# Reciprocals of three chunks spread by way of DRAM, and one tile transposed by DMA, in a fused attention and GEGLU kernel

## The chip, the cores and the metric

The kernel runs on one core of a Trainium2 chip. The metric is the device time of one execution in microseconds, as the median of several runs. A profiled run also has a span (first to last instruction, some 1.7 us shorter than the time) and the mean granted clock of TensorE. Five engines matter: TensorE (PE), VectorE (DVE), ScalarE (ACT), GpSimd (POOL) and SyncE (SP), which issues all the DMAs here.

## The reference

The input x has 2048 rows of 512 columns. It is normalized by row, then goes two ways: a dilated sliding-window attention (32 heads of 16, 8 keys at distances 0, 2, ..., 14) and a gated MLP of width 1792. The result is `x + s * silu(b)`.

```python
xn = layernorm(x)
q, k, v = split(xn @ wqkv)                       # 32 heads of 16
logits = einsum("bhsd,bhswd->bhsw", q, kg) * 16 ** -0.5   # 8 gathered keys
attn = softmax(logits);  o = einsum("bhsw,bhswd->bhsd", attn, vg)
s = o @ wo
b = (gelu(xn @ w_gate) * (xn @ w_up)) @ w_down
return x + s * silu(b)
```

## The kernel before

The rows are worked off in 4 chunks of 512. For each chunk PE runs 14 steps of gate and up projection ("glu"), then 12 steps of the next chunk's qkv projection ("qkv"), then 4 steps of the down projection and the output projection ("down"). The attention is hung onto these steps as side work by `at((stage, chunk, step), function, ...)`. Softmax divides at the end: the sums of the exponentials (`den`) are inverted into `rs`, which lies as 4 quarters of the chunk times 32 heads on the partitions, and must be spread into `rb`, in which each of 4 row groups holds the 32 heads for all 512 rows. Before the change PE does the spreading, by four matmuls with 0/1 matrices:

```python
def denominators(j):
    E = st[j]["E"]
    den = mm.tile([P, P], F32, name="den_ps", tag="mm")
    ...                                    # 8 matmuls, 32 output rows each
    nc.vector.reciprocal(out=rs[:], in_=den[:])

def spread_reciprocals(j):
    sp = mm.tile([P, TQ], F32, name="sp_ps", tag="mm")
    for q in range(4):
        nc.tensor.matmul(sp[:, q * P : (q + 1) * P], lhsT=spread[:, q, :],
                         rhs=st[j]["rs"][:], start=True, stop=True)
    rb = op.tile([P, TQ], F32, name="rb")
    nc.scalar.activation(out=rb[:], in_=sp[:], func=AF.Copy)
    st[j]["rb"] = rb

def divide(j):                             # oT = o_ps * rb, on DVE, in two halves
    ...
def down(j, tt):                           # y_ps from h and wd_sb, then s_ps from oT and wo_sb
    ...
```

The normalized rows must also be transposed (`xn` to `xnT`). Chunks 0 and 1 are transposed by PE (`transpose`: four matmuls into PSUM and a copy out of it, by ACT for six of the eight tiles), chunks 2 and 3 by DMA (`transpose_by_dma`: four DMAs of 128 x 128).

The softmax here doesn't subtract the row's maximum and nothing guards it: scores larger than these inputs give would overflow.

Of the kernel before, what the change touches and what calls it, by code (L numbers as in the profile page):

```python
# [10 lines left out]
BF16 = mybir.dt.bfloat16  # L11
F32 = mybir.dt.float32

P = 128
H = 32
# [3 lines left out]
WL = 4  # L19
WH = 2  # L20
PAD = 16
TQ = 512
# [6 lines left out]
def kernel(  # L29
# [13 lines left out]
    nc = tc.nc  # L43
    B, S, D = A_x.shape
    DF = B_w_gate.shape[1]
    NT, NC, NF, NJ = S // P, D // P, DF // P, S // TQ
    TPQ = TQ // P
# [5 lines left out]
    def pool(name, bufs, **kw):  # L53
        return ctx.enter_context(tc.tile_pool(name=name, bufs=bufs, **kw))
# [10 lines left out]
    op = pool("op", 1)  # L65
# [3 lines left out]
    dram = pool("dram", 1, space=bass.MemoryType.DRAM)  # L69
# [8 lines left out]
    wd_sb = wts.tile([P, NF, D], BF16, name="wd_sb")  # L78
    wo_sb = wts.tile([P, NC, D], BF16, name="wo_sb")
    vT = dram.tile([D, SV], BF16, name="vT")  # L80

    def load_x(t, n=1):
        nc.sync.dma_start(
            out=x_sb[:, t : t + n, :],
            in_=x2d[t * P : (t + n) * P, :].rearrange("(t p) d -> p t d", p=P),
        )
# [16 lines left out]
    def load_late_weights():  # L103
        nc.sync.dma_start(out=wd_sb[:], in_=B_w_down.rearrange("(k p) n -> p k n", p=P))
        for g in range(NC):
            nc.sync.dma_start(
                out=wo_sb[:, g, :],
                in_=bass.AP(
                    tensor=A_wo.tensor, offset=g * 4 * D, ap=[[D, 4], [DH * D, H], [1, D]]
                ),  # L110
            )
# [7 lines left out]
        out=vT.rearrange("(k p) n -> p k n", p=P)[:, :, 0:PAD],  # L119
        in_=warm[:, 0 : NC * PAD].rearrange("p (k n) -> p k n", k=NC),  # L120
# [128 lines left out]
    st = [dict(pk={}, pv={}) for _ in range(NJ)]  # L249

    def qkv(j, fo, i0=0, n=TQ, ps=None):
        which, c = divmod(fo, NC)
        if fo == 0 and i0 == 0:
            st[j]["q"] = qp.tile([P, NC, TQ], BF16, name="q_sb")
        if ps is None:
            ps = mm.tile([P, n], F32, name="qkv_ps", tag="mm")[:]
            project(ps, wqkv_sb, fo * P, j, i0, n)
        if which == 0:
            nc.scalar.activation(out=st[j]["q"][:, c, i0 : i0 + n], in_=ps, func=AF.Copy)  # L259
        elif which == 1:  # L260
            lo = PAD + j * TQ + i0
            nc.scalar.activation(out=k_sb[:, c, lo : lo + n], in_=ps, func=AF.Copy)  # L262
        else:
            vst = sm4.tile([P, TQ], BF16, name="vst")
            nc.scalar.activation(out=vst[:], in_=ps, func=AF.Copy)  # L265
            lo = PAD + j * TQ
            nc.sync.dma_start(out=vT[c * P : (c + 1) * P, lo : lo + TQ], in_=vst[:])

    def load_v(j, wls=range(WL)):

        if wls[0] == 0:
            st[j]["va"] = vap.tile([P, DH, VW], BF16, name="v_arr")
        va = st[j]["va"]
        for wl in wls:
            nc.sync.dma_start(
                out=va[H * wl : H * (wl + 1), :, :],
                in_=bass.AP(
                    tensor=vT.tensor,
                    offset=PAD + j * TQ - WL * DIL - DIL * wl,
                    ap=[[SV * DH, H], [SV, DH], [1, VW]],  # L280
                ),
            )
# [47 lines left out]
    def spread_reciprocals(j):  # L330
# [7 lines left out]
        nc.scalar.activation(out=rb[:], in_=sp[:], func=AF.Copy)  # L338
        st[j]["rb"] = rb

    def av_product(j, g, wh):
        pv = prod.tile([P, 4, TQ], BF16, name="pv", tag="prod")
        lo = WL * DIL * (1 - wh)
        nc.vector.tensor_tensor(  # L344
            out=pv[:],
            in0=st[j]["E"][:, wh, :].unsqueeze(1).to_broadcast([P, 4, TQ]),
            in1=st[j]["va"][:, 4 * g : 4 * g + 4, lo : lo + TQ],
            op=ALU.mult,
        )
        st[j]["pv"][g, wh] = pv  # L350
# [73 lines left out]
    def at(key, fn, *args):  # L424
        side.setdefault(key, []).append((fn, args))
# [5 lines left out]
    for i in range(TPQ):  # L431
        at(("qkv", 0, i), normalize, TPQ + i)
        at(("glu", 0, 7 + i), moments, 2 * TPQ + i)
        at(("glu", 0, i), transpose, TPQ + i)
        at(("glu", 0, 8 + i), normalize, 2 * TPQ + i)
        at(("glu", 1, 0), transpose_by_dma, 2 * TPQ + i)
        at(("glu", 1, 10 + i), moments, 3 * TPQ + i)
        at(("qkv", 2, 2 * i), normalize, 3 * TPQ + i)
        at(("glu", 2, 0), transpose_by_dma, 3 * TPQ + i)
# [4 lines left out]
    for i in range(8):  # L444
        at(("glu", 0, 12 + i) if i < 2 else ("qkv", 1, (0, 1, 3, 4, 5, 6)[i - 2]),
           av_product, 0, i // 2, i % 2)
    at(("qkv", 1, 3), denominators, 0)
    at(("qkv", 1, 8), spread_reciprocals, 0)
    at(("qkv", 1, 10), av_sums, 0)
    at(("qkv", 1, 10), divide, 0)  # L450

    for j in range(1, NJ):
        for w in range(W):
            early = j > 1 and w < 3
            at(("qkv", j, 9 + w) if early else ("down", j - 1, w // 3), qk_product, j, w)
        for i in range(TPQ):
            at(("down", j - 1, i), load_v, j, [i])
        at(("glu", j, 0), logits, j)
        for i in range(8):
            at(("glu", j, 2 + i), av_product, j, i // 2, i % 2)  # L460
        at(("glu", j, 11), denominators, j)
        at(("glu", j, 11), av_sums, j)
        at(("glu", j, 12), spread_reciprocals, j)
        at(("glu", j, 13), divide, j)


    HT = TPQ // 2
# [32 lines left out]
    for i in range(NC):  # L500
        run("qkv", 0, i)
        run("qkv", 0, NC + i)
        qkv(0, 2 * NC + i)
    load_v(0)
    load_late_weights()
    for j in range(NJ):
        for fc in range(NF):
            run("glu", j, fc)
# [36 lines left out]
```

## Time and profile before

| | before |
|---|---|
| time, median of 3 runs | 231.71 us (231.36 to 231.92) |
| span of the profiled run | 229.8 us |
| PE busy | 224.7 us, 98% |
| DVE, ACT busy | 64%, 58% |
| PE's waits in all | 1.5 us, all in the first 7.1 us |

The prediction shows the lines behind this table and how to read them. Two more lines are the ends of what I call PE's **stream**: from the start of the first projection (q_ps) to the start of the last group of matmuls (s_ps). The timeline of PE before (start, length, instruction group; brackets tell idle time before it and its releaser):

```profile
7.06 1.14 PE L241 MATMUL q_ps<-xnT,wqkv_sb 128*128 128x256 bf16 x9 [0.23 <-ACT xnT L216]
...
225.71 0.60 PE L409 MATMUL s_ps<-wo_sb,oT 128*128 128x256 bf16 x4
```

The stream is 225.71 - 7.06 = 218.65 us. In two more profiles of the same kernel it came out at 218.67 and 218.66 us, while its start moved between 6.81 and 7.42 us with the first loads. So the stream can be read to some 0.02 us, though the time of a run scatters by over 0.5 us.

### The profile page before, as it was taken

What the parts mean: (1) busy time and instruction counts of PE and PEld (TensorE: products, weight loads), DVE (VectorE), ACT (ScalarE), POOL (GpSimd) and SP (SyncE); (2) the same over time, 40 slices, a digit from 0 to 9 for tenths busy, and PEclk for the clock granted to TensorE, in tenths of its full rate; (3) what the DMA queues carried; (4) which work ended last, traced back from release to release, by engine and by line L of the source; (5) the groups of instructions that cost most, each with busy time, mean ns of one, the idle gap of its engine ahead of it and who ended that gap; (6) DMA issues with size and microseconds to landing.
All of it is one profiled execution on the core that took longest, in us unless ns stands there. A gap on an engine that the chain in (4) does not pass through costs nothing.

```text
span 229.8 us, 3547 instructions
## 1 busy us (share of the span) xinstructions
PE 224.7 (98%) x1339; PEld 107.6 (47%) x1339; DVE 147.5 (64%) x234; ACT 132.3 (58%) x219; POOL 20.9 (9%) x61
## 2 busy tenths in 40 slices
PE   7999999999999999999999999999999999999993
PEld 5865444444444444444444444444444444444453
DVE  5593896896995198865678169725449429945232
ACT  3779779765514867476721687646741387647211
POOL 1058924100000000110000000000000000000000
PEclk9999999999999999999999999999999999999998
DMA  6999499921288211100267611100047810000001
GB/s 156 365 374 372 109 205 200 301 81 49 85 182 198 62 27 24 26 0 0 93 163 162 146 30 23 27 11 0 27 138 160 204 30 0 0 0 4 23 23 46
DMA packets 27057, 23.71 MB, mean 103 GB/s; under 512 B 6688, under 2 KB 27040, under 8 KB 27040
## 3 DMA queue, kind: packets, MB, share of 16 engines
q1 hardware_dynamic: 27040, 23.49, 39.1%
q8 instruction: 10, 0.16, 0.3%
q14 instruction: 7, 0.06, 0.1%
HBM read 18.22 MB, written 4.21 MB: 98 GB/s over the span
## 4 chain that ended last, share of the span: by engine, by line
PE 95%; ACT 1%; DVE 1%; DMA 1%; issue 0%; DVEq 0%
PE y_ps L399 21%; PE u_ps L241 21%; PE g_ps L241 21%; PE qkv_ps L241 17%; PE s_ps L409 6%; PE L_ps L298 3%; PE o_ps L358 3%; DMA x_sb<-in_A_x_dram 1%; PE tr L207 1%; PE q_ps L241 1%; DVE stats L176 1%; ACT L383 1%; PE den_ps L318 0%; PE sp_ps L333 0%; ACT xnT L216 0%; ACT ge L383 0%
## 5 line engine op out<-in xcount | busy, mean ns | idle before, releaser
L241 PE MATMUL g_ps<-xnT,wg_sb 128*128 128x512 bf16 x224 | 57.6, 379 | 0.0
L241 PE MATMUL u_ps<-xnT,wu_sb 128*128 128x512 bf16 x224 | 57.5, 379 | 0.0
L399 PE MATMUL y_ps<-wd_sb,h 128*128 128x512 bf16 (+1 forms) x238 | 51.2, 366 | 0.0
L387 DVE TENSOR_TENSOR h<-ge,u 128x512 bf16<-128x512 bf16 x56 | 23.7, 424 | 36.6 <-ACT u L385 36.2
L287 DVE TENSOR_TENSOR pk<-q_sb,k_sb 128x2048 bf16<-128x2048 bf16 x32 | 37.8, 1220 | 8.8 <-ACT k_sb L262 8.8
L385 ACT ACTIVATE u<-u_ps 128x512 bf16<-128x512 f32 x56 | 33.5, 598 | 14.6 <-PE u_ps L241 14.5
L383 ACT ACTIVATE ge<-g_ps 128x512 bf16<-128x512 f32 x56 | 33.6, 599 | 14.0 <-PE g_ps L241 13.7
L241 PE MATMUL qkv_ps<-xnT,wqkv_sb 128*128 128x512 bf16 (+1 forms) x208 | 41.1, 355 | 0.0
L344 DVE TENSOR_TENSOR pv<-E,v_arr 128x2048 bf16<-128x2048 bf16 x32 | 38.6, 1216 | 0.0
L399 PEld LDWEIGHTS <-h 128*128 128x128 bf16 x238 | 23.3, 98 | 25.3
L406 ACT ACTIVATE sl<-y_ps 128x512 bf16<-128x512 f32 (+1 forms) x17 | 9.7, 572 | 44.0 <-PE y_ps L399 44.0
L241 PEld LDWEIGHTS <-wu_sb 128*128 128x128 bf16 x224 | 21.9, 98 | 26.6 <-issue 0.3
L241 PEld LDWEIGHTS <-wg_sb 128*128 128x128 bf16 x224 | 21.0, 98 | 26.1 <-issue 3.0
L241 PEld LDWEIGHTS <-wqkv_sb 128*128 128x128 bf16 x224 | 21.6, 98 | 19.5 <-issue 0.4
L417 DVE TENSOR_TENSOR m<-s_ps,sl 128x512 bf16<-128x512 f32 (+1 forms) x17 | 11.2, 657 | 24.2 <-PE s_ps L409 24.2
L409 PE MATMUL s_ps<-wo_sb,oT 128*128 128x512 bf16 (+1 forms) x68 | 16.6, 366 | 0.0
L192 POOL TENSOR_TENSOR rstd<-rstd,mhalf 128x1 f32<-128x1 f32 x12 | 7.7, 638 | 80.4 <-DVE rstd L189 78.2
L265 ACT ACTIVATE vst<-qkv_ps 128x512 bf16<-128x512 f32 x16 | 9.6, 597 | 6.2 <-PE qkv_ps L241 6.2
L262 ACT ACTIVATE k_sb<-qkv_ps 128x512 bf16<-128x512 f32 (+1 forms) x20 | 10.2, 516 | 3.5 <-PE qkv_ps L241 3.2
L370 DVE TENSOR_TENSOR oT<-o_ps,rb 128x1024 bf16<-128x1024 f32 x8 | 9.4, 1216 | 2.1 <-PE o_ps L358 2.1
L259 ACT ACTIVATE q_sb<-qkv_ps 128x512 bf16<-128x512 f32 (+1 forms) x16 | 8.7, 544 | 3.6 <-PE qkv_ps L241 3.3
L409 PEld LDWEIGHTS <-oT 128*128 128x128 bf16 x68 | 6.7, 98 | 7.2
(51 smaller groups left out, 120.9 us busy)
## 6 DMA issues: line engine op xcount, KB each, us to landing
v_arr<-vT SPq DMA_DIRECT2D x16, 520.0 KB, 5.2
vT<-vst SPq DMA_DIRECT2D x16, 128.0 KB, 1.7
out_dram<-o_t SPq DMA_DIRECT2D x15, 128.0 KB, 2.3
wg_sb<-in_B_w_gate_dram SPq DMA_DIRECT2D x2, 896.0 KB
wu_sb<-in_B_w_up_dram SPq DMA_DIRECT2D x2, 896.0 KB, 13.5
wd_sb<-in_B_w_down_dram SPq DMA_DIRECT2D x1, 1792.0 KB, 17.1
wqkv_sb<-in_A_wqkv_dram SPq DMA_DIRECT2D x3, 512.0 KB, 5.3
x_sb<-in_A_x_dram SPq DMA_DIRECT2D x3, 512.0 KB, 10.0
```

The costliest lines, as they stand in the source:

```text
L241: nc.tensor.matmul(ps, lhsT=w[:, dk, lo : lo + P], rhs=xnT[j][:, dk, i0 : i0 + n], start=(dk == 0), stop=(dk == NC - 1),)
L262: nc.scalar.activation(out=k_sb[:, c, lo : lo + n], in_=ps, func=AF.Copy)
L265: nc.scalar.activation(out=vst[:], in_=ps, func=AF.Copy)
L287: nc.vector.tensor_tensor(out=pk[:], in0=st[j]["q"][:], in1=k_sb[:, :, off : off + TQ], op=ALU.mult)
L344: nc.vector.tensor_tensor(out=pv[:], in0=st[j]["E"][:, wh, :].unsqueeze(1).to_broadcast([P, 4, TQ]), in1=st[j]["va"][:, 4 * g : 4 * g + 4, ...
L383: nc.scalar.activation(out=ge[:], in_=g_ps[:], func=AF.Gelu_apprx_tanh)
L385: nc.scalar.activation(out=u[:], in_=u_ps[:], func=AF.Copy)
L387: nc.vector.tensor_tensor(out=h[:], in0=ge[:], in1=u[:], op=ALU.mult)
L399: nc.tensor.matmul(y[:], lhsT=st[j][fc][:, tt * P : (tt + 1) * P], rhs=wd_sb[:, fc, cols], start=(fc == 0), stop=(fc == NF - 1),)
L406: nc.scalar.activation(out=sl[:, cols], in_=y[:], func=AF.Silu)
L409: nc.tensor.matmul(s[:], lhsT=st[j]["oT"][:, g, tt * P : (tt + 1) * P], rhs=wo_sb[:, g, cols], start=(g == 0), stop=(g == NC - 1),)
L417: nc.vector.tensor_tensor(out=m[:], in0=s[:], in1=sl[:, cols], op=ALU.mult)
```

## The change

It takes small matmuls off the bound engine and gives the work to DMAs. For chunks 0, 1 and 2 `rs` is stored to DRAM and loaded four times, once into each row group; chunk 3, which has the least time left, keeps the matmuls. The last tile of chunk 1 is transposed by DMA. The division of chunks 1 and 2 moves to a later step, so that the DRAM trip has time.

```diff
+    rs_d = [dram.tile([P, P], BF16, name=f"rs_d{j}") for j in range(NJ - 1)]
...
+    def spread_by_dma(j):
+        nc.sync.dma_start(out=rs_d[j][:, :], in_=st[j]["rs"][:])
+        rb = op.tile([P, TQ], BF16, name="rbd")
+        for i in range(WL):
+            nc.sync.dma_start(
+                out=rb[H * i : H * (i + 1), :].rearrange("h (q i) -> h q i", q=4),
+                in_=rs_d[j].rearrange("(q h) i -> h q i", h=H),
+            )
+        st[j]["rb"] = rb
...
-        at(("glu", 0, i), transpose, TPQ + i)
+        if i < TPQ - 1:
+            at(("glu", 0, i), transpose, TPQ + i)
...
     at(("qkv", 1, 3), denominators, 0)
-    at(("qkv", 1, 8), spread_reciprocals, 0)
+    at(("qkv", 1, 3), spread_by_dma, 0)
...
-        at(("glu", j, 12), spread_reciprocals, j)
-        at(("glu", j, 13), divide, j)
+        if j + 1 < NJ:
+            at(("glu", j, 11), spread_by_dma, j)
+            at(("qkv", j + 1, 6), divide, j)
+        else:
+            at(("glu", j, 12), spread_reciprocals, j)
+            at(("glu", j, 13), divide, j)
...
-    load_v(0)
-    load_late_weights()
+    at(("glu", 0, 0), transpose_by_dma, 2 * TPQ - 1)
+    at(("glu", 0, 0), load_v, 0)
+    at(("glu", 0, 0), load_late_weights)
```

## The prediction

> **What bounds the kernel now.** I read the page first: busy shares, the chain that ended last, then the waits of PE, then timelines of PE, DVE and SP around the places that the change touches. TensorE (PE) is the bound. The page says:
>
> ```profile
> PE 224.7 (98%) x1339; PEld 107.6 (47%) x1339; DVE 147.5 (64%) x234; ACT 132.3 (58%) x219; POOL 20.9 (9%) x61
> ...
> PE   7999999999999999999999999999999999999993
> ...
> PE 95%; ACT 1%; DVE 1%; DMA 1%; issue 0%; DVEq 0%
> ```
>
> The reader sees PE busy in every slice but the first and the last, and 95% of the chain on PE. A busy share alone can deceive, so the waits of PE decide:
>
> ```profile
> PE warm_ps L224 <- DVE k_sb L161: 1.1, 1, 1.1
> PE q_ps L241 <- ACT xnT L216: 0.2, 1, 0.2
> PE tr L207 <- DVE xn L198: 0.2, 1, 0.2
> ```
>
> These three are all its waits, 1.5 us of a span of 229.8 us, and all before 7.1 us. From there to the last matmul PE runs its program without a gap that the profile shows. So a change gains what it takes out of PE's stream, and loses what it makes PE wait. Work taken from ScalarE (ACT), VectorE (DVE) or the DMA queues gains nothing by itself. The places touched, in the timeline of PE:
>
> ```profile
> 17.94 0.39 PE L207 MATMUL tr<-ident,xn 128*128 128x128 bf16 x4
> 18.16 1.03 PE L241 MATMUL g_ps<-xnT,wg_sb 128*128 128x512 bf16 x4
> 19.03 1.03 PE L241 MATMUL u_ps<-xnT,wu_sb 128*128 128x512 bf16 x4
> ...
> 52.40 0.39 PE L333 MATMUL sp_ps<-rs,spread 128*128 128x128 bf16 x4
> 52.62 1.67 PE L241 MATMUL qkv_ps<-xnT,wqkv_sb 128*128 128x512 bf16 x7
> ```
>
> The durations overlap because matmuls are pipelined; the price of a group is the distance to the next start. Four transposes cost 18.16 - 17.94 = 0.22 us, four spreading matmuls 52.62 - 52.40 = 0.22 us, 55 ns each, not the 219 ns that the groups list as the mean of one. A 512-column matmul costs (19.03 - 18.16) / 4 = 0.22 us.
>
> **What the Trainium skill says.** "TensorE: Matmul & The Clock Gate", section "Back-to-back issue gap", gives an isolated gap of about 56 ns at 128 columns and 216 ns at 512, and for real streams of weight load and matmul 81 and 131 ns. This trace has 55 and 218 ns in a real stream, so I use the trace, which agrees with the first pair. "Perfetto Trace Analysis", section "Identifying the Most-Contended Engine", says that matmul busy time is a bad measure of the distance to the best possible time; agreed here, since 219 ns of "duration" cost 55 ns, and I therefore use starts and waits. "DMA: Bandwidth & Descriptors", section "Anatomy of one DMA", puts a fixed cost of about 2 us on a transfer (there for the GpSimd path), most of it the write's receipt; here stores of 128 KB land in 1.7 us and DMA transposes in 2.3 us, which agrees roughly. The same page, section "Why a DMA increments its semaphore by 16 and not by 1", says that the slowest dimension of the access pattern sets how many of 16 DMA engines a transfer uses. The loads of wo_sb have an outer dimension of 4; in the table by stretches the DMA share of 46 to 50 us, when they are what is left, is 0.29 and 0.27, near 4 of 16. Agreed; it matters below.
>
> **The change, part by part.**
>
> (a) Removed from PE: four spreading matmuls for each of chunks 0, 1 and 2, 3 x 0.22 = 0.66 us, and four transposes of the last tile of chunk 1, 0.22 us. Sum 0.88 us, all on the path, as PE never waits there. The denominators stay, chunk 3 stays.
>
> (b) Removed from ACT: three copies of sp_ps to rb at 0.591 us and one of tr to xnT at about 0.59 us, 2.4 us in all. ACT is 58% busy and PE waits for it once, for 0.2 us: worth 0.
>
> (c) The division now reads a bf16 rb beside o_ps in PSUM. I keep its 1.215 us: a choice. For chunks 1 and 2 it moves from the 14th GLU step into the QKV stage, where DVE idles for 3.25 us ahead of the first product of q and k (109.69 us). Worth 0 to PE.
>
> (d) Added to the SP queue: per chunk one store of 32 KB to DRAM, a wait until it has landed, and four loads of 32 KB. Estimate from stores of this trace (0.33 us of issue, 1.7 us to landing): 1.7 for the store, then four issues of about 0.38 us, the last landing about 2 us after its start: 1.7 + 3 x 0.38 + 2.0 = 4.9 us from rs to a full rb, call it 5 to 6 with semaphores. For chunk 1 rs is ready at 97.7 us (reciprocal 96.74 + 0.95) and SP has finished issuing its 16 transposes at 97.3 us (75.44 + 21.86). rb is full near 103.5; the division is due at about 107, and oT is used at about 115. Hidden by over 5 us. Chunk 2 is alike. Chunk 0 is the tight one:
>
> ```profile
> 50.06 0.95 DVE L327 RECIPROCAL rs<-den_ps 128x128 bf16<-128x128 f32 x1
> 50.92 3.42 DVE L344 TENSOR_TENSOR pv<-E,v_arr 128x2048 bf16<-128x2048 bf16 x3
> ...
> 56.47 2.36 DVE L370 TENSOR_TENSOR oT<-o_ps,rb 128x1024 bf16<-128x1024 f32 x2 [2.12 <-PE o_ps L358]
> 58.74 3.49 DVE L287 TENSOR_TENSOR pk<-q_sb,k_sb 128x2048 bf16<-128x2048 bf16 x3
> ...
> 58.02 3.19 PE L399 MATMUL y_ps<-wd_sb,h 128*128 128x512 bf16 x14
> 61.04 1.03 PE L409 MATMUL s_ps<-wo_sb,oT 128*128 128x512 bf16 x4
> ```
>
> rs is ready at 51.0, so rb is full at 51.0 + 5 to 6 = 56 to 57 us. The division already waits until 56.47 for o_ps, so it starts 0 to 0.5 us later and ends by 58.8 to 59.4. PE wants oT for s_ps at 60.8 (first weight load of oT), 60.4 with the gain of two groups. Slack 1.0 to 1.6 us: hidden, narrowly.
>
> (e) Added: four DMA transposes at the head of the GLU stage, ahead of the loads of v_arr, wd_sb and wo_sb. They are read only by its QKV stage at 45 us, some 17 us after they should land. They take SP about 1.23 us each, 4.9 us. But SP has a hole there:
>
> ```profile
> 17.71 3.94 SPq L267 DMA_DIRECT2D vT<-vst  x4
> 27.20 1.31 SPq L275 DMA_DIRECT2D v_arr<-vT  x2
> ```
>
> From 21.65 to 27.20 it waits for the stores of vT to land (the longest wait of that kind is 5.4 us). The transposes fill that hole, with the last of them bound to the landing of the small store to vT by a shared semaphore. I expect v_arr to be issued 0 to 2 us later, say 1. Those loads run at full DMA share until 44 us and wo_sb trails on a few engines until 51 us, so with 1 us more the trail ends at 52 us, and the store of rs (51.0) could sit behind it for up to 1 us.
>
> The sum: -0.88 from PE, about +0.05 for a small chance of a stall at s_ps: 231.71 - 0.83 = 230.9 us.
>
> **The rivals.** *Rival 1, a wait takes the place:* late v_arr loads delay the first products pv (43.71 us; the last v_arr lands near 29.2 + 12.9 = 42.1 us, so 1.6 us of slack), or wo_sb's trail delays rs, and rb comes over 1.2 us too late. PE then stands at s_ps of the first down tile. For it: slack of one microsecond, a queue at full share, 256-byte pieces. Against it: the DMA share of 52 to 54 us is 0.00, so rb's own traffic meets nothing. It would eat 0.5 to 2 us: 231.2 to 232.5. *Rival 2, nothing is gained:* freed PE time is lost where PE later meets ACT or DVE. For it: products pv of chunk 0 end at 54.35 while o_ps starts at 54.44, so DVE is close behind. Against it: the last product is needed only by the last eighth of o_ps, about 1.5 us later, and the trace shows no wait. It would leave 231.7. *Rival 3, more is gained:* fewer uses of the PSUM ring and of ACT remove hidden stalls. Against it: no stall shows after 7.1 us. It would need 227 us to be "faster by over 2%", 5 times what was taken out.
>
> **Range and chances.** Centre 230.9. The three runs before spread over 231.36 to 231.92, 0.3 us each way; with all of the gain and a lucky run 230.2; with rival 1 at some 1.2 us, 232.0. Two per cent are 4.6 us, five times the gain and over twice what rival 1 can eat: faster 0.01, same 0.96, slower 0.03.
>
> **What would show it.** PE's count falls by 16 to 1323 and its busy time by about 0.9 us; the rows of sp_ps shrink to 4 matmuls, those of tr to 28. The waits of PE stay at the same three: step (a) right. A new line "s_ps waits for DVE oT", or DVE's oT waiting for a DMA of rbd by over 2 us, would show rival 1; a wait of o_ps for pv would show rival 1 by v_arr, or rival 2. oT at 1.2 us shows (c) right; the v_arr issue near 28 us shows (e) right. I am wrong if the round trip by DRAM takes over 7 us in chunk 0, if the transposes stall the queue for much over 2 us, or if PE's 55 ns were partly shade of its neighbours, so that less than 0.88 us comes out.

## The result

The changed kernel took 230.26 us (median of 6 runs, 230.10 to 230.59), the kernel before beside it 231.74 us (6 runs). The ratio is 0.9941, with a 95% interval of 0.9928 to 0.9954: "same" at 2%, and inside the stated range, though only 0.06 us above its low end. A ratio here is the mean time of one kernel's fast runs over that of the other's of the same rounds, so it is not quite the ratio of the medians. The gain is larger than foreseen: 1.4 us by the ratio, where I had 0.83.

The page of the changed kernel, the same three lines as were read before:

```profile
PE 222.7 (97%) x1303; PEld 106.8 (47%) x1323; DVE 147.6 (65%) x234; ACT 130.6 (57%) x215; POOL 21.7 (10%) x61
...
PE   7999999999999999999999999999999999999994
...
PE 94%; ACT 2%; DVE 1%; DMA 1%; issue 1%; ACTq 0%; DVEq 0%
```

The weight loads (PEld) count 1323, 16 fewer, as they must. Matmuls count only 1303: 20 records are missing from this trace, so its busy sum is not used. (In two more profiles of the changed kernel, e4_again and e9_after_third below, they count 1323, as expected.) PE is the bound as before. All its waits in the changed kernel:

```profile
PE warm_ps L225 <- DVE k_sb L162: 1.1, 1, 1.1
PE tr L208 <- DVE xn L199: 0.3, 1, 0.3
PE g_ps L242 <- issue: 0.2, 1, 0.2
```

No wait of s_ps for oT or of o_ps for pv has come. (The 0.2 us of "issue" stands where a matmul's record is missing.) The ends of the stream in the timeline of PE after, and chunk 0 between them:

```profile
7.15 1.03 PE L242 MATMUL q_ps<-xnT,wqkv_sb 128*128 128x256 bf16 x8
...
47.94 6.22 PE L242 MATMUL qkv_ps<-xnT,wqkv_sb 128*128 128x512 bf16 x28
54.09 1.91 PE L370 MATMUL o_ps<-pv,hsum 128*32 128x512 bf16 x32
...
60.69 1.03 PE L421 MATMUL s_ps<-wo_sb,oT 128*128 128x512 bf16 x4
...
224.91 0.60 PE L421 MATMUL s_ps<-wo_sb,oT 128*128 128x256 bf16 x4
```

The stream is 224.91 - 7.15 = 217.76 us, 0.89 us shorter than before, against 0.88 from 55 ns a matmul. The run of qkv_ps before o_ps is no longer cut by sp_ps.

The part that came close to going wrong is chunk 0's trip by DRAM. First SP's queue, then DVE's timeline, both after:

```profile
21.57 6.09 SPq L234 DMA_TRANSPOSE xnT<-xn  x4
27.83 2.65 SPq L276 DMA_DIRECT2D v_arr<-vT  x4
...
50.92 0.33 SPq L344 DMA_DIRECT2D rs_d<-rs  x1
52.76 1.75 SPq L347 DMA_DIRECT2D rbd<-rs_d  x4
```

```profile
49.94 0.95 DVE L328 RECIPROCAL rs<-den_ps 128x128 bf16<-128x128 f32 x1
...
57.89 2.36 DVE L382 TENSOR_TENSOR oT<-o_ps,rbd 128x1024 bf16<-128x1024 f32 x2 [3.66 <-PE qkv_ps L242]
```

The transposes fill SP's hole as thought, and v_arr is issued 0.63 us later (27.20 before). But the division starts at 57.89, not at 56.5 to 57, and ends at 60.25. PE takes its first weights of oT at 60.5 us. The slack is 0.25 us, not the 1.0 to 1.6 I had worked out; in e4_again and e9_after_third, two more profiles of this kernel, it is some 0.65 us. (The bracket blames qkv_ps. PE does end that group near then, but the division reads nothing of it; in both these profiles the same wait carries the name of rbd.)

The trace also keeps every DMA packet and every count of a semaphore, and they show which part was late. A load counts its semaphore up in 16 parts. Of the last of the four loads, 15 parts had landed by 55.87 us and the 16th at 57.76. The page lists a DMA queue of another kind beside that of the kernel's own transfers:

```profile
q8 instruction: 10, 0.16, 0.3%
```

These are ten fetches of program code, 16 KB each. One ran from 55.19 to 56.56 us, and the last 8 of the 512 packets of 256 bytes of the four loads started at 56.55, as it ended. Ten profiles have this trip with a fetch near it. In six (this one, e3, e4, e6, e9, e11) the loads were still under way when the fetch began, and the last load was complete 2.7 to 3.7 us after its issue. In the other four (e2, e5, e7, e8) its packets went out before the fetch could hold them or after it had ended, and it took 1.7 to 1.8 us. DVE's timeline of e2_spread_only, where the division waits for o_ps alone:

```profile
56.25 2.36 DVE L382 TENSOR_TENSOR oT<-o_ps,rbd 128x1024 bf16<-128x1024 f32 x2 [1.85 <-PE o_ps L370]
```

So the delay goes with the fetch. That both ran on one DMA engine is inferred from the times, since the records don't name the engine, and no run moved the fetch.

Chunk 1 in the timelines of SP and of DVE, after:

```profile
97.36 0.33 SPq L344 DMA_DIRECT2D rs_d<-rs  x1
98.82 1.74 SPq L347 DMA_DIRECT2D rbd<-rs_d  x4
```

```profile
103.90 2.35 DVE L382 TENSOR_TENSOR oT<-o_ps,rbd 128x1024 bf16<-128x1024 f32 x2
```

There is no bracket: the division came to its turn and found rb full (its last part had landed at 102.02 us, 4.7 us after rs was ready). It takes 1.2 us a half with a bf16 rb, as with f32.

### The profile page after: what moved, and what is told of

Same layout as the page of the kernel before. It is cut to its first block, busy times and chain, and to the rows that moved or that the text cites. A ratio compares the mean times of both kernels' runs of the same rounds, so it can differ in the third digit from the quotient of the medians.

```text
span 228.8 us, 3516 instructions
## 1 busy us (share of the span) xinstructions
PE 222.7 (97%) x1303; PEld 106.8 (47%) x1323; DVE 147.6 (65%) x234; ACT 130.6 (57%) x215; POOL 21.7 (10%) x61
## 4 chain that ended last, share of the span: by engine, by line
PE 94%; ACT 2%; DVE 1%; DMA 1%; issue 1%; ACTq 0%; DVEq 0%
PE y_ps L411 21%; PE u_ps L242 21%; PE g_ps L242 20%; PE qkv_ps L242 17%; PE s_ps L421 6%; PE L_ps L299 3%; PE o_ps L370 3%; DMA x_sb<-in_A_x_dram 1%; PE q_ps L242 1%; PE tr L208 1%; DVE stats L177 1%; ACT L395 1%; ACT u L397 1%; PE den_ps L319 0%; ACT xnT L217 0%
## 5 line engine op out<-in xcount | busy, mean ns | idle before, releaser
L242 PE MATMUL g_ps<-xnT,wg_sb 128*128 128x512 bf16 x214 | 56.5, 379 | 0.6 <-issue 0.2
L242 PE MATMUL qkv_ps<-xnT,wqkv_sb 128*128 128x512 bf16 (+1 forms) x203 | 40.5, 354 | 0.2
L382 DVE TENSOR_TENSOR oT<-o_ps,rbd 128x1024 bf16<-128x1024 f32 x6 | 7.1, 1219 | 3.7 <-PE qkv_ps L242 3.7
```

Source lines behind the costliest of these rows:

```text
L242: nc.tensor.matmul(ps, lhsT=w[:, dk, lo : lo + P], rhs=xnT[j][:, dk, i0 : i0 + n], start=(dk == 0), stop=(dk == NC - 1),)
```

## The experiments

**The theories.** The first timing gains 1.4 us, the stream only 0.89. Theory A: what leaves PE's stream is the gain, and the rest is scatter at the two ends. Theory B: a removed group is worth more than its 0.22 us. Theory C: part of the gain lies outside PE's stream. A second set of runs asks how near the change came to losing its gain.

Twelve experiments ran, some of them copies of the two kernels; all gave correct results. "Granted" in the table means runs at a granted clock of 0.999 or more. Some runs of several kernels, the one before among them, were at 0.993 and took about 2 us more (231.6 and 233.6 us for the same kernel), though they count as fast. They widen the intervals of the ratios, so I compare medians and the means of the granted runs. All runs of the table were on one chip, except the last row's.

| run | what it is | median, us | mean of granted runs, us (number) | PE stream, us |
|---|---|---|---|---|
| e0_control, e10_control_again and before | kernel before | 231.54 | 231.51 (19) | 218.65 to 218.67 |
| e1_transpose_only | transpose alone | 231.22 | 231.19 (5) | 218.44 |
| e2_spread_only | reciprocals alone | 230.92 | 230.78 (3) | 218.04 |
| e3_put_back | changed, 16 matmuls put back | 231.41 | 231.43 (3) | 218.67 |
| e4_again, e9_after_third | changed kernel | 230.36 | 230.32 (9) | 217.77, 217.76 |
| e5_hop0 | second trip, chunk 0 | 232.35 | 232.10 (4) | 219.58 |
| e6_hop1 | second trip, chunk 1 | 230.50 | 230.64 (4) | 217.76 |
| e8_eight | two tiles by DMA | 234.59 | 233.96 (1) | 221.96 |
| e7_all4 | all four chunks, early denominators | 231.21 | 231.24 (6) | 218.19 |
| e11_best | all four chunks, other chip | 230.47 | 230.46 (2) | 217.54 |

### e0_control and e10_control_again: what a difference means that means nothing

No edit.

> A copy of the kernel before, timed against the kernel before. Every theory expects 1.000; what it shows instead is the size of a difference that means nothing. I expect 0.999 to 1.001, under 0.25 us.

> The copy of the kernel before a second time, beside the runs of the changed kernel on the same chip. Every theory: 1.000, with a scatter of 0.2 us.

Measured: medians of 231.40 and 231.66 us beside 231.61, ratios 0.9976 (0.9938 to 1.0014) and 0.9985 (0.9946 to 1.0024). So on medians of six runs 0.25 us means nothing, and the ratios, pulled by the slow-clock runs among before's, are good to some 0.4% only.

### e1_transpose_only and e2_spread_only: the two parts alone

```diff
 # e1: the kernel before, with only
+        if i < TPQ - 1: at(("glu", 0, i), transpose, TPQ + i)
+    at(("glu", 0, 0), transpose_by_dma, 2 * TPQ - 1)     # then load_v(0), load_late_weights
 # e2: the changed kernel, with only that undone
```

> The kernel before with the DMA transpose of the last tile of chunk 1 alone. Theory A (the gain is what leaves PE's stream, 0.22 us a group of four 128-column matmuls): 0.22 us less, ratio 0.9990. Theory B (a group taken out is worth more than the distance of starts shows, some 0.35 us): 0.35 us less. Theory C (part of the 1.4 us gain lies outside PE, at the start or the end, or came with the order of the early loads, which only this part changes): 0.5 us or more less.

> The changed kernel with the transpose put back on PE, so the reciprocals by way of DRAM alone. Theory A: 0.66 us less than before, ratio 0.9972. Theory B: 1.05 us less, ratio 0.9955. Theory C, if the early loads are behind the rest: 0.66 us; if it sits with this part: 0.9 us or more.

Measured: streams of 218.44 us (0.21 to 0.23 below the kernel before) and 218.04 us (0.61 to 0.63 below, where 0.66 was expected from starts read to 0.01 us). Together they make 0.84 of the 0.89 us of the whole change, so nearly all. Theory B is refuted for the stream: a group costs what the distance of starts says. In time, the granted runs are 0.32 and 0.73 us below, each 0.1 more than its stream, within the scatter. The ratios, 0.9967 and 0.9969 with intervals that reach 1, decide nothing.

### e3_put_back: the removed matmuls issued again for nobody

```diff
 # the changed kernel, with its DMAs, and
+    at(("glu", 0, 3), idle_transpose, 2 * TPQ - 1)   # 4 transposes into a tile that nobody reads
+    at(("qkv", 1, 8), idle_spread, 0)                # 4 spreading matmuls, likewise
+            at(("glu", j, 12), idle_spread, j)       # chunks 1 and 2
```

> The changed kernel with the 16 removed 128-column matmuls issued again at their old places, their results read by nobody. Theories A and B (all of the gain is PE's stream): as the kernel before, ratio 0.999 to 1.001, and PE's first to last matmul takes 218.6 us in the profile as before. Theory C (part of the gain lies elsewhere): still 0.4 to 0.6 us below the kernel before.

Measured: a stream of 218.67 us, the same as before to 0.02, and a median of 231.41 us, that of e0_control. With the DMAs in place and the copies of ACT still gone, the gain in the stream is gone once PE has its matmuls back. That is the strongest evidence for theory A, and it shows that the ACT copies were worth nothing to the stream. (One small piece of the gain lies at the end of the kernel, see the next experiment. It is still there in this run: from the last s_ps to the end takes 3.86 us, as in the changed kernel. In the time, 0.08 us below the kernel before on the granted runs, it can't be told from scatter.)

### e4_again and e9_after_third: is it 0.9 or 1.4?

No edit to the changed kernel.

> The changed kernel once more, on another chip or at another time. PE's stream from the first q_ps to the last s_ps is 0.89 us shorter in the profile (218.65 to 217.76), yet the first timing says 1.37 us. Theory A (PE's stream is all; the rest is scatter of the start and of the last store between runs): 0.6 to 1.1 us below before, ratio near 0.996. Theory C (the changed kernel also starts or ends earlier, always): 1.3 us or more again, ratio 0.994.

> The changed kernel a third time, for the question whether its gain is the 0.89 us of PE's stream or the 1.4 us of the first timing. Theory A: over all runs at a granted clock of 0.999 or more it stays 0.8 to 1.1 us below the copies of the kernel before. Theory C: 1.3 us or more.

Measured: medians of 230.24 and 230.42 us, streams of 217.77 and 217.76. The nine granted runs average 230.32, those of the kernel before 231.51 (19 runs): 1.19 us less, between the two theories' figures. One more piece is in the profile, the wait of SP for the last store at the very end. Before and after, from the waits of SP:

```profile
SPq L540 <- DMA out_dram<-o_t: 1.1, 1, 1.1
```

```profile
SPq L558 <- DMA out_dram<-o_t: 0.9, 1, 0.9
```

It was 1.1 us in all three profiles of the kernel before and 0.9 in all three of the changed one. So from the last s_ps to the end it takes 4.02 to 4.09 us before and 3.87 to 3.89 after, some 0.16 us less. Stream and end make 1.05 of the 1.19 us. The last 0.14 us is less than the scatter of the start (6.76 to 7.43 us over all profiles) and within the noise of the two means (1.19 give or take 0.16, estimated from the scatter of the runs), and stays open. I had predicted nothing at the end: theory C is right for this small piece.

### e5_hop0 and e6_hop1: how much room the DRAM trip has

```diff
         rs = st[j]["rs"]
+        if j == 0:            # e6_hop1: j == 1
+            nc.sync.dma_start(out=rs_h[:, :], in_=rs[:])
+            rs = sm2.tile([P, P], BF16, name="rs_b")
+            nc.sync.dma_start(out=rs[:], in_=rs_h[:, :])
         nc.sync.dma_start(out=rs_d[j][:, :], in_=rs[:])
```

> The changed kernel with a second round trip by DRAM for the reciprocals of chunk 0. In the profile of the changed kernel oT of chunk 0 is done at 60.25 us and PE takes it at 60.5. Theory of the narrow slack: the extra trip of about 3.7 us makes PE wait at s_ps of the first down tile by 2.3 to 3.7 us, and the time is that much over the changed kernel (232.5 to 234). Rival (the wait in front of oT was not rb's, or the stages behind have room): under 0.5 us over it.

> The same second round trip for chunk 1 in place of chunk 0. By my estimate rb of chunk 1 has over 5 us of room up to its use, so the time is that of the changed kernel within 0.3 us and PE has no new wait. Rival (any lengthening of the DRAM trip shows): 2 us or more over it.

For e5_hop0, one line of PE's waits, one of DVE's timeline, and two of PE's timeline:

```profile
PE s_ps L427 <- DVE oT L388: 1.5, 2, 0.9
```

```profile
60.28 2.36 DVE L388 TENSOR_TENSOR oT<-o_ps,rbd 128x1024 bf16<-128x1024 f32 x2 [6.29 <-DMA rbd<-rs_d]
```

```profile
61.57 0.60 PE L427 MATMUL s_ps<-wo_sb,oT 128*128 128x512 bf16 x2 [0.93 <-DVE oT L388]
62.70 0.61 PE L427 MATMUL s_ps<-wo_sb,oT 128*128 128x512 bf16 x2 [0.52 <-DVE oT L388]
```

The division is held by rbd, by name, and starts 2.4 us later than in the changed kernel. PE waits for each half of oT. The stream grows by 1.82 us, and the granted runs by 1.8 (232.10 against 230.32; four runs from 231.03 to 232.66). The direction and the place are as foreseen; the size fell short of the 2.3 to 3.7 expected, for two reasons. The loads went out 4.3 us later (57.09 against 52.76), but they missed the code fetch, which had held the last of them by 1.9 us in the changed kernel, so rb was full only 2.4 us later. And PE starts on the first half of oT while DVE makes the second. In e6_hop1 the stream stays at 217.76 us with no new wait of PE: chunk 1 has the room. (Its granted runs are 0.3 us above the changed kernel; its wait for the last store is 1.1 us again, and its four runs range over 1 us.)

### e8_eight: one tile more into the hole of the queue

```diff
-        if i < TPQ - 1:
+        if i < TPQ - 2:
             at(("glu", 0, i), transpose, TPQ + i)
+    at(("glu", 0, 0), transpose_by_dma, 2 * TPQ - 2)
     at(("glu", 0, 0), transpose_by_dma, 2 * TPQ - 1)
```

> The changed kernel with two tiles of chunk 1 (eight transposes) by DMA ahead of v_arr, not one. Theory of the hole (SP waits 5.5 us for vT there, room for four transposes of 1.23 us): v_arr is issued some 5 us later, near 33 us, the first product pv starts 3 to 4 us late, and PE waits at o_ps of chunk 0 for 1.5 to 3 us, less 0.22 us for the group taken out: 231.5 to 233. Rival (transposes beside the loads are hidden anyway): 0.22 us below the changed kernel.

SP's timeline, DVE's timeline and PE's waits of this run:

```profile
21.60 11.19 SPq L234 DMA_TRANSPOSE xnT<-xn  x8
32.84 2.73 SPq L276 DMA_DIRECT2D v_arr<-vT  x4
```

```profile
47.70 1.23 DVE L356 TENSOR_TENSOR pv<-E,v_arr 128x2048 bf16<-128x2048 bf16 x1 [3.99 <-DMA v_arr<-vT]
```

```profile
PE o_ps L370 <- DVE pv L356: 2.2, 3, 0.7
```

The chain is the one foreseen, link by link: transposes past the hole, v_arr 5 us later, pv 4 us later, PE waiting 2.2 us at o_ps. Yet the stream grew by 4.2 us, not by some 2. The rest is in the table by stretches of time. Its columns are the stretch and its length, PE busy (records), PEld busy, DVE busy, ACT busy and POOL busy, then the granted clock, the DMA share and GB/s:

```profile
56.00:58.00 2.00, 0.80 (x8) 0.20 (x8) 2.00 (x3) 0.00 (x0) 0.00 (x0) 1.00 0.16 48
58.00:60.00 2.00, 1.60 (x8) 0.65 (x8) 0.34 (x1) 0.00 (x0) 0.00 (x0) 0.74 0.19 45
60.00:62.00 2.00, 2.00 (x7) 0.64 (x5) 0.96 (x1) 0.60 (x1) 0.00 (x0) 0.50 0.52 161
62.00:64.00 2.00, 2.00 (x10) 0.88 (x9) 2.00 (x3) 1.80 (x2) 0.00 (x0) 0.91 0.34 116
```

In the 2 us in which PE waited most (busy for 0.80 of 2.00) the clock was still full; after it, it fell. The 0.74 and 0.91 are means over parts: with stretches cut at 58.94 and 62.35 us the clock is 0.50 between them and 1.00 on both sides, so PE ran at half clock for 3.4 us, which cost 1.7 us. The starts of the groups close the account. From o_ps to the next qkv_ps it takes 58.73 - 54.16 = 4.57 us, against 55.93 - 54.09 = 1.84 in the changed kernel: 2.73 us for the waits (more than the 2.2 us of idle time, which is counted from modelled ends of matmuls). From there to s_ps it takes 6.44 against 4.76 us: 1.68 for the clock. Together they are 4.41 us, which is the 4.2 us and the 0.22 of the group taken out.

The Trainium skill, "TensorE: Matmul & The Clock Gate", section "What's actually happening", describes a gate that falls to 4/8 after an idle window of about 3.4 us, and its section "A second HAM failure mode: psum-queue depth-cycling" tells of frequent short idle times between groups of matmuls with the same effect. The trace agrees with the level (0.50) and with the second section: no single wait here was longer than 0.73 us. In e5_hop0, with waits of 0.93 and 0.52 us, the clock stayed at 1.00. Nor does the half clock come in every run of e8_eight: the profiled one took 235.22 us at a mean clock of 0.992, and the one at 1.000 took 233.96 us, still 3.6 us above the changed kernel. The waits alone are a clear loss.

### e7_all4: the fourth chunk too, with early denominators

```diff
-    at(("qkv", 1, 3), denominators, 0)
-    at(("qkv", 1, 3), spread_by_dma, 0)
+    at(("glu", 0, 12), denominators, 0)
+    at(("glu", 0, 12), spread_by_dma, 0)
...
-        at(("glu", j, 11), denominators, j)          # beside av_sums
+        at(("glu", j, 5), denominators, j)           # alone, for every chunk from 1 to 3
+        at(("glu", j, 5), spread_by_dma, j)
         at(("glu", j, 11), av_sums, j)
```

> A version meant to beat both: the reciprocals of all four chunks by way of DRAM, with the denominators taken as soon as E is there (five GLU steps in, for chunk 0 in the 13th GLU step of its own chunk), so that chunk 3 has time for the trip too; the constants of the spreading matmuls fall away. By the price of PE's stream one more group of four leaves: stream of 217.54 us from first q_ps to last s_ps against 217.76 for the changed kernel, time 0.2 us below it, no new wait of PE. Rival: the store of chunk 0, now waiting in the SP queue behind the loads of wo_sb or ahead of the stores of vT, or that of chunk 3, makes PE wait at s_ps, and the time is 0.5 us or more above it.

A miss. No wait of PE came, but the stream was 218.19 us, 0.65 us more than the 217.54 expected, and the granted runs were at 231.24 us. PE's timeline tells why. First the changed kernel, where the denominators stand beside the sums o_ps:

```profile
93.28 1.03 PE L242 MATMUL u_ps<-xnT,wu_sb 128*128 128x512 bf16 x4
94.24 0.29 PE L319 MATMUL den_ps<-E,hsum 128*32 128x128 bf16 x8
94.36 1.90 PE L370 MATMUL o_ps<-pv,hsum 128*32 128x512 bf16 x32
96.19 1.04 PE L242 MATMUL g_ps<-xnT,wg_sb 128*128 128x512 bf16 x3
```

Then e7_all4, where they stand apart:

```profile
82.88 1.03 PE L234 MATMUL u_ps<-xnT,wu_sb 128*128 128x512 bf16 x4
83.84 0.29 PE L311 MATMUL den_ps<-E,hsum 128*32 128x128 bf16 x8
84.07 1.04 PE L234 MATMUL g_ps<-xnT,wg_sb 128*128 128x512 bf16 x4
...
93.57 1.03 PE L234 MATMUL u_ps<-xnT,wu_sb 128*128 128x512 bf16 x4
94.53 1.91 PE L362 MATMUL o_ps<-pv,hsum 128*32 128x512 bf16 x32
96.37 1.04 PE L234 MATMUL g_ps<-xnT,wg_sb 128*128 128x512 bf16 x4
```

A group u_ps takes 0.865 us to the next group of its kind. Beside each other, den and o_ps cost 96.19 - 93.28 - 0.865 = 2.05 us. Apart they cost 84.07 - 82.88 - 0.865 = 0.32 and 96.37 - 93.57 - 0.865 = 1.94, so 2.26. That is 0.21 us for each of three chunks, 0.63 of the 0.65 us missed. What differs is the step from matmuls with 128 output rows to those with 32 (128*128 and 128*32 in the lines) and back, which e7_all4 makes twice as often. The Trainium skill, "TensorEngine Tiling (Array Packing)", section "Key Properties", says that changing the tiling mode drains TensorE. The trace agrees that such a step costs, without any wait being shown for it; that it is a drain is the page's word, not shown here. The next run puts the two groups beside each other again, and the cost is gone.

### e11_best: the version that the runs point to

```diff
+        early = 1 if j + 1 == NJ else 0
+        at(("glu", j, 11 - early), denominators, j)      # beside av_sums again
+        at(("glu", j, 11 - early), av_sums, j)
+        at(("glu", j, 11 - early), spread_by_dma, j)     # all four chunks
+        at(("glu", j, 13) if early else ("qkv", j + 1, 6), divide, j)
...
-        nc.sync.dma_start(out=wd_sb[:], ...)
+        for lo, hi in ((0, 4), (4, 8), (8, 11), (11, NF)):
+            nc.sync.dma_start(out=wd_sb[:, lo:hi, :], ...)
```

> What the eleven runs point to. The last spreading group (chunk 3) goes by DRAM too, but its denominators stay beside the sums of the products (one GLU step earlier than before, both together), because standing alone a group of denominators cost 0.32 us of PE's stream and beside the sums 0.11. And the load of wd_sb is cut in four, which adds three DMAs and so puts the last store of the output back on the semaphore of the highest number, as in the changed kernel. Expected: stream 217.54 us (0.22 below the changed kernel), the wait for the last store 0.9 us if that wait goes with the semaphore's number and 1.1 us if it is otherwise tied to the changed kernel; time 230.1 us, 0.2 us below the changed kernel's 230.3. Rival: chunk 3's trip by DRAM is too long and PE waits at s_ps, or the pieces of wd_sb delay rs of chunk 0 behind wo_sb: 230.6 us or more.

The stream was 217.54 us, to the digit. The waits of SP show the end:

```profile
SPq L551 <- DMA out_dram<-o_t: 0.9, 1, 0.9
```

DMAs take eight semaphores in turn. Counting in the instruction streams, the last store has the highest of them (7) in the changed kernel, in e3_put_back and here, and these wait 0.9 us. It has another (0, 1, 3 or 4) in the kernel before, e1, e2, e5, e6, e7 and e8, and these wait 1.1 us. So the 0.16 us at the end goes with the number of DMAs before it, and could be moved there on purpose. The last instructions of SP in the traces show why. The last store lands 3.03 us after the start of the last s_ps in the kernel before and 3.02 in the changed one, so the difference comes after it. SP checks the eight semaphores in a fixed order, one step each 0.06 us, with number 7 in the last step. In the kernel before it is released at number 4 (228.75 us) and has three more steps to pass; in the changed kernel it is released at the last (227.95 us).

In time, the median was 230.47 us beside 231.56 for before, ratio 0.9959 (0.9945 to 0.9972). The 230.1 us expected were not reached, and the rival's 230.6 neither. This was another chip, so it is not compared with the changed kernel's 230.36. The version beats the kernel before; that it beats the changed one is shown for the stream (0.22 us) only, not for the time.

## Why the prediction was right, and where it was not

- **PE bounds, and its stream is what counts: right.** e3_put_back shows it from the other side: with the matmuls back, nothing of the stream's gain is left. Not all of the time is in the stream, though: 0.16 us came at the end.
- **Step (a), 0.88 us: right.** The stream lost 0.89 us; 0.22 of it is the transpose (e1) and 0.62 the reciprocals (e2, expected 0.66).
- **Steps (b) and (c), ACT and the division worth nothing: right.** e3_put_back has both and is as slow as before; a half of the division still takes 1.2 us.
- **Step (d), the DRAM trip hidden: right in the outcome, for chunk 0 by a narrow margin.** The trip itself was priced well. Undisturbed it took 4.6 us from rs to a full rb (e2_spread_only, chunk 0: 51.05 to 55.69 us) and 4.7 and 4.8 us (chunks 1 and 2 of the changed kernel), against the estimate of 4.9. The wrong step is "rb's own traffic meets nothing". It was argued from the DMA share of 52 to 54 us, while the loads run until 56. There the last load met a code fetch, and rb was full 6.9 us after rs. The division started at 57.89 us in place of 56.5 to 57, and the slack at s_ps was 0.25 us in place of 1.0 to 1.6. That this was still enough is partly luck: the sign of being wrong that the prediction names, a trip of over 7 us in chunk 0, was missed by 0.1 us. In e2_spread_only, with loads issued 0.2 us sooner, the packets were out by 55.33 us, the fetch began at 55.35, and the division waited for o_ps alone. For chunks 1 and 2 the step was right; only chunk 1 was tested by a longer trip (e6_hop1).
- **A sign that was badly chosen.** "DVE's oT waiting for a DMA of rbd by over 2 us" was to show rival 1. It came true in e4_again and e9_after_third (3.2 us each) without any wait of PE. The view puts the whole idle time down to what came last, and some 2 us of it are the wait for o_ps that was there before.
- **Step (e), the hole in SP's queue: right.** v_arr came 0.63 us later, "0 to 2, say 1" was expected. (The four transposes held SP for 6.1 us and not 4.9.) e8_eight shows that the hole is full with one tile.
- **The rivals.** Rival 1, a wait in place of the work, did not occur, but it was near: 2.4 us more of delay made it true (e5_hop0), and e8_eight made its other form true. Rivals 2 and 3 fell.
- **The centre.** I took 0.83 us off; measured were 1.4 at first and 1.19 over all granted runs on one chip. The range held for the first timing by 0.06 us, at the end that I had kept for a lucky run, so the fit of the number says less than the fit of the stream (0.89 against 0.88). Missing was a term for the end of the kernel (0.16 us), which depends on the number of DMAs, and 0.14 us which no experiment places.

## What to carry to other kernels

When one engine runs without a gap, price what leaves it by the distance of starts in its own stream, and check a gain by the length of that stream, which can be read to 0.02 us where times scatter by 0.5. A transfer that takes over the work is free only up to the slack of the place where its result is used, and the smallest slack decides; look there for a hole in the issuing queue, don't fill it twice, and ask what else the DMA engines carry up to the landing, code fetches too. Keep matmuls of one tile shape together: each small group moved away from its kind cost 0.21 us of PE time, nearly what a group of spreading matmuls saves (0.22).

## What the Trainium skill lacked or had wrong

- "TensorE: Matmul & The Clock Gate", section "Back-to-back issue gap": for real streams of weight load and matmul it gives 81 ns at 128 columns and 131 ns at 512. The runs show 55 and 218 ns in such a stream, near the isolated figures of the same section.
- The same page, section "Why this matters for your kernels", asks for no PE gaps over some 3 us, and its section on the second failure mode gives no size for the short ones. In e8_eight three gaps of 0.7 us within 3 us were followed by half clock for 3.4 us, which cost 1.7 us beside the 2.7 of the waits; two gaps of 0.9 and 0.5 us (e5_hop0) were not.
- "TensorEngine Tiling (Array Packing)", section "Key Properties", says that a change of tiling mode drains TensorE but gives no price. Here a lone group of 32-row matmuls between 128-row ones cost 0.21 us more than the same group beside others of its kind (0.32 against 0.11 us).
- No page that I read tells that the end of a kernel depends on which semaphore the last store has: 0.9 against 1.1 us of waiting, the same in each profile of a kernel.
- No page that I read gives what a code fetch costs a data transfer that it meets: here 16 KB in 0.9 to 1.4 us, and a load of 32 KB that took 2.7 to 3.7 us in place of 1.7 to 1.8.
